# Attention beside a feed-forward product: the keys in chunks of 128 with 64 left over, and the left-over ones in four quadrants of the tensor engine

## The chip, the cores and the metric

One core of one Trainium2 chip. The metric is the device time of one execution in microseconds (us), medians of several runs. Where two kernels are compared, the ratio is the mean time of the one's fast runs over the mean of the other's fast runs in the same rounds, so it is not quite the ratio of the medians quoted.

## The reference, cut to what matters

```python
q, k, v: (8, 12, 448, 64)                      # batch, heads, sequence, head size; all float32
q_n, k_n = rmsnorm(q, g_q), rmsnorm(k, g_k)
attn = softmax(q_n @ k_n.T / sqrt(64))         # 448 x 448 for each head
x = (attn @ v) arranged to (3584, 768)
h = x @ w_in                                   # first product, to 2048 columns
out = relu(h)**2 @ w_out                       # second product, back to 768
```

## The kernel before

Two batches make a span, four spans in all; a span has twelve pairs of heads. The attention of span 0 runs alone. The attention of each later span runs beside the second product of the span ahead of it: Python generators deal out the matmuls of both, in one order for the tensor engine (PE). These three stretches are what the change touches. The products use a scheme with seven multiplications in place of eight, for which VectorE also forms sums and differences ("combine"). In span 0 it does so during the first eight products of the stretch.

The parts that matter, cut:

```python
NJ, SP = 4, 112                                   # 448 keys = 4 chunks of 112

def scores(i, c):                                 # later spans; keys on the partitions
    sc = ps_s.tile([SP, 2, 512], F32, tag="s")    # PSUM: 2 x 2 banks
    for h in range(2):                            # two heads, two row tiles of 64
        nc.tensor.matmul(sc[:, h, 0:S], qkT[rows(h), 0, 1, chunk c], qkT[rows(h), 0, 0, :])
    nc.scalar.activation(probs[i, c], sc[:, :, 0:S], AF.Exp)

def values(i):
    pavs[i] = ps_o.tile([P, S], F32, tag="o")     # one bank
    for c in range(NJ):
        for h in range(2):                        # two heads, two column tiles of 64
            nc.tensor.matmul(pavs[i][rows(h), :], vs[i][:, h, c, :], probs[i, c][:, h, :], ...)

def attention(first):                             # one turn for each pair, beside the second product
        scores(i, 0); scores(i, 1)
        values(i - 1)
        spread(i - 1)                             # ScalarE's queue: load the factors back, 1/sum of each query
        add_up(i, 1)                              # VectorE: row sums, chunk on chunk
        scores(i, 2); scores(i, 3)
        norm_by_squares(i + 2); yield             # VectorE and GpSimd
        transposes(i + 1); yield
        add_up(i, 2); add_up(i, 3)
        finish(i - 1); yield                      # VectorE: x = values * factors; frees bank "o"
        fold(i)                                   # VectorE: sum over partitions, reciprocal
        combine_x(i - 1); yield
        nc.sync.dma_start(factors in DRAM, ...)   # SyncE's queue: store the factors
        yield

# second product, one output block of eight matmuls:
ps = ps_o.tile([P, S], F32, tag="t") if j % 3 == 2 else bank("ps")    # three banks in turn
```

All eight PSUM banks are in use: four for the scores, "o" for the values, and "t" and two of `bank` for the second product.

## Time and profile before

| | |
|---|---|
| time, median of the first four runs | 1403.36 us |
| span in the profile | 1399.7 us |
| TensorE busy | 99% at a mean granted clock of 0.998 |
| the three stretches beside the second product | 207.4 us each |

A stretch is read from the trace: from the first score matmul of its twelve pairs to the first matmul of the next first product. The table of stretches has it as follows (length; then busy time of PE, PEld, DVE, ACT, POOL, each with its count; granted clock, DMA share, GB/s):

```profile
263.22:470.64 207.42, 207.42 (x721) 90.94 (x721) 159.53 (x303) 59.13 (x73) 83.76 (x42) 1.00 0.54 116
597.37:804.78 207.41, 207.41 (x721) 90.94 (x721) 144.18 (x275) 58.02 (x72) 82.85 (x43) 1.00 0.54 116
931.51:1138.93 207.42, 207.42 (x721) 90.94 (x721) 145.24 (x275) 57.91 (x72) 83.98 (x43) 1.00 0.51 111
```

PE is busy for the whole of each; no wait shows. VectorE (the third busy time) has 15 us more to do in the first, the combinations.

### The profile page before, as it was taken

The page shows a single profiled execution, that of the slowest core. Times are in us where ns is not written, and L with a number is a line of the kernel's source. Part 1 is how long each engine was busy: PE and PEld are TensorE (multiplying, and loading weights), DVE is VectorE, ACT ScalarE, POOL GpSimd, SP SyncE. Part 2 cuts the span into 40 slices and gives each one's busy share as a digit, 9 for nine tenths or more (in the row PEclk, how much of TensorE's full clock was granted, in tenths as well). Part 3 has the DMA queues.
Part 4 walks back from the last instruction along what each step waited for, and adds up shares of the span by engine and source line. Part 5 has one row for each costly group of instructions (what it writes and reads, how often), then busy time and mean ns, then how long its engine had stood idle before and what let it go on. Part 6 is the DMA issues. An engine that isn't in the chain of part 4 may idle for free.

```text
span 1399.7 us, 14445 instructions
## 1 busy us (share of the span) xinstructions
PE 1379.2 (99%) x4450; PEld 638.5 (46%) x4450; DVE 802.2 (57%) x1398; ACT 419.6 (30%) x621; POOL 581.7 (42%) x400
## 2 busy tenths in 40 slices
PE   8989999999999999999999999999999999999997
PEld 3333455444444454544444455444444445554553
DVE  6889676589876234476777523457777633332111
ACT  7875556432322011233332011233333201110000
POOL 5998877444552123544453122544445302221000
PEclk9999999999999999999999999999999999999999
DMA  9687998545764332344665333344564332334443
GB/s 240 189 229 199 341 384 306 143 97 120 144 121 105 102 90 85 104 113 110 127 130 119 97 94 90 98 106 105 129 126 102 95 101 85 90 87 104 106 111 70
DMA packets 430915, 188.79 MB, mean 135 GB/s; under 512 B 277484, under 2 KB 428780, under 8 KB 430828
## 3 DMA queue, kind: packets, MB, share of 16 engines
q1 hardware_dynamic: 421228, 179.05, 49.8%
q10 hardware_dynamic: 9472, 8.72, 2.3%
q8 instruction: 38, 0.62, 0.2%
q14 instruction: 49, 0.40, 0.1%
q0 software_dynamic: 128, 0.00, 0.0%
HBM read 154.54 MB, written 33.16 MB: 134 GB/s over the span
## 4 chain that ended last, share of the span: by engine, by line
PE 93%; POOL 3%; DVE 1%; DMA 1%; ACT 1%; issue 1%; ACTq 0%; POOLq 0%
PE ps L1047 37%; PE sc L749 10%; PE pd L1000 10%; PE pa L1000 10%; PE pc L1000 10%; PE pav L805 9%; PE pb L1000 5%; PE tot L819 1%; POOL rstd L697 1%; POOL gC L563 1%; DMA sw<-w1s 1%; POOL gC L569 1%; PE pt L737 0%; ACT gT L754 0%; POOL qk L699 0%
## 5 line engine op out<-in xcount | busy, mean ns | idle before, releaser
L1047 PE MATMUL ps<-gT,sw 128*128 128x448 f32 x768 | 299.2, 543 | 0.8 <-POOL gT L977 0.8
L719 POOL TENSOR_TENSOR half<-half,mhalf 128x28 f32<-128x28 f32 x36 | 173.6, 4822 | 266.9 <-DVE half L718 226.8
L1047 PE MATMUL ps<-gC,sw 128*128 128x448 f32 x576 | 225.2, 543 | 0.0
L977 POOL TENSOR_TENSOR gT<-gT 128x448 f32<-128x448 f32 x96 | 94.9, 990 | 309.9 <-ACT gT L973 309.9
L1047 PEld LDWEIGHTS ps<-gT,sw 128*128 128x128 f32 x768 | 144.1, 190 | 150.7 <-issue 147.0
L756 ACT ACTIVATE pr<-sc 112x896 f32<-112x896 f32 x120 | 104.7, 914 | 293.4 <-PE sc L749 184.9
L749 PE MATMUL sc<-qkT 64*112 64x448 f32 x768 | 170.6, 563 | 0.9 <-ACT qkT L383 0.8
L1047 PEld LDWEIGHTS ps<-gC,sw 128*128 128x128 f32 x576 | 108.2, 190 | 112.1 <-issue 110.8
L1000 PE MATMUL pa<-xT,sw 128*128 128x448 f32 x384 | 154.9, 540 | 0.0
L973 ACT ACTIVATE gT<-gT 128x448 f32<-128x448 f32 x96 | 55.3, 577 | 310.1 <-DVE gT L1015 310.0
L749 PEld LDWEIGHTS sc<-qkT 64*112 64x112 f32 x768 | 61.2, 173 | 97.9 <-issue 81.3
L1000 PEld LDWEIGHTS pa<-xT,sw 128*128 128x128 f32 x384 | 73.0, 190 | 71.6 <-issue 70.3
L805 PE MATMUL pav<-pr,vt 112*64 112x448 f32 x480 | 100.2, 547 | 0.0
L721 POOL TENSOR_TENSOR qk<-qk,half 128x448 f32<-128x448 f32 x72 | 81.3, 1150 | 2.8
L764 DVE TENSOR_TENSOR acc<-acc,pr 112x896 f32<-112x896 f32 x60 | 68.2, 1136 | 21.0 <-ACT pr L756 18.5
L1000 PE MATMUL pb<-xC,sw 128*128 128x448 f32 x192 | 77.6, 540 | 1.5 <-issue 1.5
L1000 PE MATMUL pd<-xT,sw 128*128 128x448 f32 x192 | 77.9, 542 | 0.0
L1000 PE MATMUL pc<-xC,sw 128*128 128x448 f32 x192 | 77.5, 540 | 0.2 <-DMA sw<-w1s 0.2
L1000 PE MATMUL pd<-xC,sw 128*128 128x448 f32 x192 | 77.5, 540 | 0.0
L1000 PE MATMUL pc<-xT,sw 128*128 128x448 f32 x192 | 77.4, 539 | 0.0
L1015 DVE TENSOR_TENSOR gT<-z,pd 128x448 f32<-128x448 f32 x32 | 19.8, 620 | 99.7 <-PE pd L1000 99.7
L569 POOL TENSOR_TENSOR gC<-gC 128x384 f32<-128x384 f32 x64 | 72.8, 1157 | 2.5
(120 smaller groups left out, 1551.0 us busy)
## 6 DMA issues: line engine op xcount, KB each, us to landing
sw<-w1s SPq DMA_DIRECT2D x224, 192.0 KB, 2.3
sw<-w2s SPq DMA_DIRECT2D x168, 256.0 KB, 3.3
w1s<-gC SPq DMA_DIRECT2D x8, 1344.0 KB, 7.5
w2s<-gC SPq DMA_DIRECT2D x8, 1344.0 KB, 7.6
out_dram<-osb SPq DMA_DIRECT2D x184, 56.0 KB, 1.9
qk<-in_q_dram SPq DMA_DIRECT2D x144, 56.0 KB, 3.0
qk<-in_k_dram SPq DMA_DIRECT2D x144, 56.0 KB, 2.9
vt<-in_v_dram SPq DMA_DIRECT2D x72, 112.0 KB, 2.9
```

Source lines behind the costliest of these rows:

```text
L569: nc.gpsimd.tensor_tensor(*[blocks_of(n)[:, i] for i in (dst, x, y)], op)
L719: nc.gpsimd.tensor_tensor(half, half, mhalf, ALU.pow)
L721: nc.gpsimd.tensor_tensor(qkn[:, s], raw[:, s], half[:, s * NG:(s + 1) * NG].rearrange("p g -> p g ()").to_broadcast([P, NG, 32]), ALU.mult)
L749: nc.tensor.matmul(sc[:, h, 0:S], qkT[rows, at, 1, c * SP:(c + 1) * SP], qkT[rows, at, 0, :], start=True, stop=True)
L756: nc.scalar.activation(pr, sc[:, :, 0:S], AF.Exp)
L764: nc.vector.tensor_tensor(acc, probs[i, 0] if c == 1 else acc, probs[i, c], ALU.add)
L805: nc.tensor.matmul(pavs[i][h * D:(h + 1) * D, :], vs[i][:, h, c, :], probs[i, c][:, h, :], start=(c == 0), stop=(c == NJ - 1))
L973: nc.scalar.activation(g, src, AF.Relu)
L977: nc.gpsimd.tensor_tensor(g, g, g, ALU.mult)
L1000: nc.tensor.matmul(ps, stream[n + i][:, c], rhs[:, c], start=first and c == 0, stop=c == HC - 1, skip_group_check=not first)
L1015: add(g, x, ps, ALU.add)
L1047: nc.tensor.matmul(ps, stream[n][:, c % 4], rhs_of[i][:, c], start=c == 0, stop=c == HF - 1)
```

## The change

The intent: 4 chunks of 112 keys leave rows of the array empty. Three full chunks of 128 and a rest of 64 need fewer steps, if the rest costs half a step: its 64 keys by 64 values fill a quarter of the array, so two heads times two halves of the queries can run at once in the four quadrants. The halves of the queries land on two row tiles, and their values in two banks, so the second half has a bank ("t") of its own and is joined to the first later. The diff, cut (asserts, loads and buffer sizes left out):

```diff
 def load_v(i):
-    for h in range(2):
-        nc.sync.dma_start(vs[i][:, h], v[b, h0 + h].rearrange("(j p) d -> p j d", j=NJ))
+    for h in range(2):
+        nc.sync.dma_start(vs[i][:, h, 0:NF], v[b, h0 + h, 0:NF * P].rearrange("(j p) d -> p j d", j=NF))
+    for rows in sides:        # the last 64 keys twice, on partitions 0-63 and 64-127
+        nc.sync.dma_start(vs[i][rows, :, NF], v[b, h0:h0 + 2, NF * P:].rearrange("h p d -> p h d"))
 def scores(i, c):
+    n = S if c < NF else S // 2
+    for h in range(2):
+        for m in range(S // n):
+            part = slice(0, P) if c < NF else sides[m]
+            nc.tensor.matmul(sc[part, h, 0:n], qkT[rows, 0, 1, c * P:min((c + 1) * P, S)],
+                             qkT[rows, 0, 0, m * n:(m + 1) * n], start=True, stop=True)
 def add_up(i, c):
+    if i >= NAT and c == NF:
+        for m, rows in enumerate(sides):
+            part = acc[rows, :, m * S // 2:(m + 1) * S // 2]
+            nc.vector.tensor_tensor(part, part, probs[i, c][rows], ALU.add)
+        return
+def later_values(i):          # after the three full chunks
+    rests[i] = ps_o.tile([P, S], F32, tag="t", name="rest")
+    for h in range(2):
+        for m, rows in enumerate(sides):
+            into = rests[i] if m else pavs[i]
+            nc.tensor.matmul(into[h * D:(h + 1) * D, 0:S // 2], vs[i][rows, h, NF, :],
+                             probs[i, NF][rows, h, :], start=bool(m), stop=True)
 def finish(i):
+    half = pav[:, S // 2:]
+    nc.vector.tensor_tensor(half, half, rests.pop(i), ALU.add)
     nc.vector.tensor_tensor(x, pav, factors, ALU.mult)
 def attention(first):
-    scores(i, 2)
-    scores(i, 3)
+    scores(i, 3)
+    scores(i, 2)
+    nc.scalar.copy(rest, rests[i - 1][:, 0:S // 2])
 # second product
-    ps = ps_o.tile([P, S], F32, tag="t", name="ps") if j % 3 == 2 else bank("ps")
+    ps = bank("ps")
```

## The prediction

> **What bounds the kernel now.** I read the page's engine rows first, then the 40 slices, the chain that ended last, the timeline of TensorE, and last the timeline of ScalarE where an eviction was late.
>
> ```profile
> PE 1379.2 (99%) x4450; PEld 638.5 (46%) x4450; DVE 802.2 (57%) x1398; ACT 419.6 (30%) x621; POOL 581.7 (42%) x400
> ```
>
> ```profile
> PE  8989999999999999999999999999999999999997
> ...
> PEclk9999999999999999999999999999999999999999
> ```
>
> TensorE is busy for 1379.2 of 1399.7 us at full clock, and after the first few slices never idle. The chain that ended last is 93% PE. So only TensorE time counts, plus any wait that the change newly puts in front of TensorE. The change touches the stretches in which attention for the next two batches runs between the matmuls of the second product (L1047): three stretches of 12 head pairs. One such period, from the timeline of TensorE (start, length, engine, line, operation, count):
>
> ```profile
> 643.93 1.76 PE L749 MATMUL sc<-qkT 64*112 64x448 f32 x8
> 645.62 2.48 PE L805 MATMUL pav<-pr,vt 112*64 112x448 f32 x12
> 647.93 0.92 PE L805 MATMUL pav<-qkT,vt 112*64 112x448 f32 x4
> 648.78 1.76 PE L749 MATMUL sc<-qkT 64*112 64x448 f32 x8
> 650.47 7.03 PE L1047 MATMUL ps<-gT,sw 128*128 128x448 f32 x18
> 657.34 3.17 PE L1047 MATMUL ps<-gC,sw 128*128 128x448 f32 x8
> 660.44 1.76 PE L749 MATMUL sc<-qkT 64*112 64x448 f32 x8
> ```
>
> From start to start: scores of chunks 0 and 1 take 645.62 - 643.93 = 1.69 us, values 648.78 - 645.62 = 3.16, scores of chunks 2 and 3 1.69, the 26 records of L1047 9.97. Every matmul leaves two records. Read record by record, starts in steady state are 0.3757 us apart for 448 columns. In the scores (64 rows, two row tiles) and the values (64 columns, two column tiles) the two heads' records start 5 to 7 ns apart, so a pair costs one step of 0.3757. Take those steps off and a fixed part is left where the shape of the tiles changes: scores 1.69 - 4 x 0.3757 = 0.19, values 3.16 - 8 x 0.3757 = 0.15, L1047 9.97 - 26 x 0.3757 = 0.20.
>
> **What the Trainium skill says.** (1) "FP8 and Floating Point Precision", TensorE Precision Notes: true FP32 takes four passes through the array. The trace agrees: two records of 0.3757 us for 448 columns, 0.75 us a matmul. (2) "TensorEngine Tiling (Array Packing)", Tiling Modes, Key Properties: changing the tiling mode drains TensorE, changing the tile does not, and a 64x64 mode has four independent tiles. The trace has the drain, 0.15 to 0.20 us a change; no run here yet has the four tiles. (3) "TensorE: Matmul & The Clock Gate", Part 3: Packing small matmuls: tiles start about 4 ns apart and run at once. The trace shows 5 to 7 ns for two tiles. (4) "PSUM — Partial Sum Buffer", PSUM bank collisions raise a hardware error: different row tiles may not write one bank at the same time. No run shows it, but it is why the change needs a bank of its own for the second half of the queries.
>
> **The change, part by part.** Beside the second product the 448 keys go as 3 x 128 + 64 instead of 4 x 112.
>
> *Removed:* one of four chunks, in scores and in values: 2 x 2 steps of 0.3757 = 1.503 us of a pair's 6.01.
>
> *Added:* the 64 keys left over, in scores and in values, as four matmuls of 64x64x224, one to a quadrant. If all four run at once, a set is two steps of 224 columns, about 0.3757/2 = 0.189 us each: 0.378 us a set, 0.756 for both. The weight loads of 64 columns took 136 ns in the values, less than a step of 189, so they should hide as now.
>
> *Mode changes:* the order is scores 0 and 1 (64x128), values 0 to 2 (128x64), left-over values and then left-over scores (both 64x64, hence the swap of chunks 2 and 3), scores 2 (64x128), L1047. That is five changes in place of four: about +0.15 us, as for the other 64-column mode.
>
> So a period with both parts: -1.503 + 0.756 + 0.15 = -0.60 us. 11 such periods a stretch, 33 in all: -19.7 us. The first pair of a stretch has scores alone and the last period values alone: each -0.752 + 0.378 + 0.15 = -0.22, six in all, -1.3. **Together -21.0 us on TensorE.**
>
> *Other engines.* VectorE: the last addition becomes two of 64 partitions by 448, at 0.62 each (the mean of its 128x448 additions) in place of one of about 1.12, +0.1; joining the halves, 224 wide, is 0.39 by the slope between 448 (0.617) and 896 (1.081). So +0.5 us a period. ScalarE: an exponential of half the size saves about 0.37, a copy of 224 columns costs about as much (both estimates from its 448-wide rows of 0.53 to 0.58). GpSimd loses three clears of 0.84. SyncE issues two more transfers of v per pair, near 0.5 us each. None is on the chain unless it delays something for TensorE:
>
> ```profile
> 268.37:453.00 184.63, 184.63 (x647) 80.70 (x647) 151.44 (x290) 55.67 (x69) 82.05 (x39) 1.00 0.55 118
> 602.52:787.50 184.98, 184.98 (x647) 80.90 (x648) 135.19 (x260) 55.13 (x69) 80.63 (x39) 1.00 0.55 117
> ```
>
> (The table of stretches: length, then busy time of PE, PEld, DVE, ACT, POOL.) VectorE was busy for 151 of 185 us in the first stretch and would be for about 157 of 178: 89%, not a bound on the mean.
>
> *Moved: a bank.* The products of L1047 rotated over three banks and now have two, since the third ("t") holds the left-over values. A product of eight matmuls is 6.0 us of TensorE, so an eviction must now be over before the next product ends, not the one after. For all 84 products I compared the end of the eviction with the start of the product two later. Nearly all have 2 to 12 us to spare. Three do not, the same product (the fifth) in each stretch, because its copy is on ScalarE:
>
> ```profile
> 321.56 1.11 ACTq L785 DMA_DIRECT2D xT<-factors  x2
> 322.78 1.72 ACT L756 ACTIVATE pr<-sc 112x896 f32<-112x896 f32 x2 [7.87 <-PE ps L1047]
> 324.39 0.54 ACT L1056 COPY p<-ps 128x448 f32<-128x448 f32 x1
> ```
>
> ```profile
> 654.39 1.11 ACTq L785 DMA_DIRECT2D xT<-factors  x2
> 655.60 1.72 ACT L756 ACTIVATE pr<-sc 112x896 f32<-112x896 f32 x2 [8.84 <-issue]
> 657.21 0.54 ACT L1056 COPY p<-ps 128x448 f32<-128x448 f32 x1
> ```
>
> ScalarE stood some 8 us ahead of these transfers of the factors. The copies end at 324.93 and 657.75; the products two later start at 323.19 and 657.34 (the L1047 line above). With two banks TensorE would have waited 1.7 and 0.4 us, and with periods 0.6 us shorter 2.3 and 1.0. In the third stretch 1.0 us was to spare, 0.4 would be left. I charge **+3.4 us**.
>
> The sum: 1403.6 - 21.0 + 3.4 = **1386 us**, 1.3% faster.
>
> **The rivals.**
>
> *A: the quadrants do not run four at a time.* Each of the four matmuls has two records on its own quadrant, and the second must follow the first. If the queue does not look past three waiting second passes, the tiles start one after another: five steps of 0.189 a set in place of two, +0.57 us, times 72 sets = +41 us: 1427 us. If only two run together, four steps, +0.38, +27 us: 1413. One at a time, eight steps, +1.13, +82: 1468. For it: each column half reads its own stream from the same rows and no trace here has four tiles; 16 loads and matmuls must start in 0.38 us, four times as densely as in the values. Against it: with two tiles the first pass of the second head starts 5 ns after that of the first head and ahead of its second pass, in row and in column tiles alike, and the transposes (L737) start a load and a matmul every 94 ns, which is their array time. I give the cases of A together about 15%.
>
> *B: a wait takes the place.* VectorE goes near its limit in the first stretch, lags, and holds up the two banks, or ScalarE delays the exponentials that free the scores' banks. For it: 89% busy, and a late eviction now stops TensorE. Against: at the score banks the trace leaves about 2.7 us between the end of an exponential and the matmul that needs its bank, and the new order takes only 0.2 to 0.6 of it. B would make 5 to 12 us of waits instead of 3.4: 1388 to 1395.
>
> *C: no waits and cheap changes of mode:* 1403.6 - 21.0 = 1382.6, or 1380 with a smaller drain.
>
> **The range and the chances.** The mechanism alone gives 1383, the bank 1386, B up to 1395, the mild half of A about 1400. Range 1381 to 1401. Over 2% faster means under 1375.5, which even all the removed work without a new change of mode (36 x 0.75 = 27 us, 1376.7) does not reach: 3%. Over 2% slower means above 1431.7, only with quadrants run nearly in turn: 4%. Within 2%: 93%.
>
> **What would show each step right or wrong.** In the timeline of TensorE: the left-over values as eight records over about 0.4 to 0.55 us from their start to that of the left-over scores, and those about 0.38 us to the start of scores 2; record starts in fours a few ns apart. If they start in twos or singly, A holds. The L1047 records keep their 0.3757 us, and a period falls from 16.5 to 15.9 us (15.76 to 15.16 with 24 records). Idle time of TensorE ahead of L1047, released by ScalarE's copy L1056's counterpart, of 2 to 4 us in all shows the lost bank; more, or released by VectorE, shows B. The prediction is wrong in its mechanism if the three stretches together do not shorten by 15 to 22 us.

## The result, and the profile after

| | before | after |
|---|---|---|
| median (first four runs) | 1403.36 us | 1393.22 us (1391.20 to 1396.39) |
| ratio, 95% interval | | 0.9935 (0.9911 to 0.9959) |
| span in the profile | 1399.7 us | 1389.0 us |

The time lies in the range, 7 us above the central value. The page's first row and the table of stretches, after:

```profile
PE 1360.9 (98%) x4738; PEld 636.1 (46%) x4738; DVE 829.7 (60%) x1470; ACT 418.0 (30%) x657; POOL 572.1 (41%) x397
```

```profile
263.59:470.79 207.20, 201.93 (x818) 89.92 (x818) 170.03 (x327) 58.13 (x85) 82.01 (x41) 1.00 0.55 118
597.48:799.73 202.25, 201.14 (x817) 90.11 (x817) 153.66 (x299) 57.65 (x84) 79.06 (x42) 1.00 0.55 121
926.44:1127.97 201.53, 201.15 (x818) 90.16 (x818) 153.64 (x299) 57.70 (x84) 79.86 (x42) 1.00 0.52 116
```

The three stretches came from 622.3 to 611.0 us, 11.3 shorter: 0.2 in the first, 5.2 in the second, 5.9 in the third. So the question is why the first gained nothing.

The timeline of PE shows that the quadrants work (start, length, engine, line, operation, shapes, count):

```profile
678.52 1.67 PE L834 MATMUL pav<-pr,vt 128*64 128x448 f32 x8
680.13 0.40 PE L840 MATMUL pav<-half,vt 64*64 64x224 f32 x1
680.13 0.40 PE L840 MATMUL rest<-half,vt 64*64 64x224 f32 x1
680.14 0.40 PE L840 MATMUL pav<-half,vt 64*64 64x224 f32 x1
680.15 0.40 PE L840 MATMUL rest<-half,vt 64*64 64x224 f32 x1
680.37 0.35 PE L840 MATMUL pav<-half,vt 64*64 64x224 f32 x1
...
680.56 1.51 PE L758 MATMUL sc<-qkT 64*64 64x224 f32 x12
682.00 5.53 PE L1089 MATMUL ps<-gT,sw 128*128 128x448 f32 x14
```

Four records start within 20 ns (5 to 7 ns apart, read record by record), then the four second passes together, and 0.19 us later the left-over scores begin, with no change of tile shape between. An undisturbed turn of attention (scores, values, left-over keys, without L1089) takes 5.98 us; before it took 6.54.

Where the rest went, in the first stretch. Two kinds of waits are new. The first stands ahead of the values:

```profile
308.92 1.77 PE L758 MATMUL sc<-qkT 64*128 64x448 f32 x8
312.83 1.73 PE L834 MATMUL pav<-pr,vt 128*64 128x448 f32 x8 [2.14 <-DVE xT L877]
```

In square brackets is the idle time and what ended it: the multiplication that empties the values' bank for the pair two turns back. VectorE (DVE) at that time:

```profile
307.92 1.08 DVE L784 TENSOR_TENSOR acc<-acc,qkT 128x896 f32<-128x896 f32 x1
309.04 2.65 DVE L782 TENSOR_TENSOR acc<-acc,half 64x448 f32<-64x448 f32 x2
311.72 0.40 DVE L876 TENSOR_TENSOR pav<-pav,half 128x224 f32<-128x224 f32 x1
312.16 0.62 DVE L877 TENSOR_TENSOR xT<-pav,xT 128x448 f32<-128x448 f32 x1
```

It works without a gap, one instruction after another: it is simply late. GpSimd (POOL) at that time:

```profile
304.11 4.80 POOL L724 TENSOR_TENSOR half<-half,mhalf 128x28 f32<-128x28 f32 x1 [11.47 <-DVE half L723]
308.99 2.22 POOL L726 TENSOR_TENSOR qk<-qk,half 128x448 f32<-128x448 f32 x2
```

The same place in the kernel before, where the multiplication (L839) ended 0.55 us before the values began:

```profile
308.75 1.64 DVE L764 TENSOR_TENSOR acc<-acc,qkT 112x896 f32<-112x896 f32 x1
310.32 0.61 DVE L839 TENSOR_TENSOR xT<-pav,xT 128x448 f32<-128x448 f32 x1
```

```profile
311.48 0.97 PE L805 MATMUL pav<-pr,vt 112*64 112x448 f32 x4
```

After the change the scores behind the values in the same turn were late too, by some 0.6 us in all. They wait for ScalarE's exponentials, which free their banks; and these had waited for a step of `fold` on VectorE (L793):

```profile
315.01 1.73 ACT L761 ACTIVATE pr<-sc 128x896 f32<-128x896 f32 x2 [6.22 <-DVE quarters L793]
```

```profile
316.79 1.02 PE L758 MATMUL sc<-qkT 64*128 64x448 f32 x4 [0.20 <-ACT pr L761]
```

The second kind is ahead of the seventh product, for its bank:

```profile
322.86 1.13 ACTq L805 DMA_DIRECT2D xT<-factors  x2
...
325.55 0.57 ACT L1098 COPY p<-ps 128x448 f32<-128x448 f32 x1
```

```profile
326.21 3.25 PE L1089 MATMUL ps<-gC,sw 128*128 128x448 f32 x8 [1.44 <-POOL half L724]
```

The bracket names GpSimd, but the copy on ScalarE ends at 326.12 and the matmul starts 0.1 us later, in each of the three stretches: that is the bank it waits for.

To weigh the waits I took each turn and each block of L1089 in the trace and subtracted its undisturbed length (5.98 us a turn; 0.3757 us a record plus 0.20 a block). The first stretch waits 2.84 and 1.73 us in the turns in which the values were late (the idle time ahead of the values alone is 2.14 and 1.03; some 0.6 of each lies ahead of the scores that follow) and 1.68 for the bank; the second 1.38 and the third 0.65 for the bank. With trifles, 8.4 us in all. Without them each stretch is 200.87 us, so TensorE was spared 3 x 6.55 = 19.6 us, and 19.6 - 8.4 = 11.2.

### The profile page after: what moved, and what is told of

It is laid out like the page before. It is cut to its first block, busy times and chain, and to the rows that moved or that the text cites. A ratio compares the mean times of both kernels' runs of the same rounds, so it can differ in the third digit from the quotient of the medians.

```text
span 1389.0 us, 15124 instructions
## 1 busy us (share of the span) xinstructions
PE 1360.9 (98%) x4738; PEld 636.1 (46%) x4738; DVE 829.7 (60%) x1470; ACT 418.0 (30%) x657; POOL 572.1 (41%) x397
## 4 chain that ended last, share of the span: by engine, by line
PE 85%; DVE 6%; POOL 3%; issue 2%; DMA 2%; ACT 2%; SPq 1%; ACTq 0%; POOLq 0%
PE ps L1089 33%; PE pd L1042 10%; PE pa L1042 10%; PE pc L1042 10%; PE sc L758 7%; PE pav L834 5%; PE pb L1042 5%; PE sc L767 1%; PE pav L840 1%; PE tot L854 1%; PE pav L826 1%; POOL rstd L702 1%; DMA sw<-w1s 1%; POOL gC L566 1%; DMA factors<-square 1%
## 5 line engine op out<-in xcount | busy, mean ns | idle before, releaser
L1089 PE MATMUL ps<-gT,sw 128*128 128x448 f32 x768 | 299.2, 543 | 0.8 <-POOL gT L1019 0.8
L724 POOL TENSOR_TENSOR half<-half,mhalf 128x28 f32<-128x28 f32 x36 | 173.6, 4822 | 267.6 <-DVE half L723 249.3
L1089 PE MATMUL ps<-gC,sw 128*128 128x448 f32 x576 | 225.5, 543 | 2.9 <-ACT p L1098 1.5
L1089 PEld LDWEIGHTS ps<-gT,sw 128*128 128x128 f32 x768 | 144.1, 190 | 149.3 <-issue 145.2
L1089 PEld LDWEIGHTS ps<-gC,sw 128*128 128x128 f32 x576 | 107.9, 190 | 115.8 <-issue 108.4
L758 PE MATMUL sc<-qkT 64*128 64x448 f32 (+1 forms) x720 | 118.8, 484 | 0.7 <-ACT pr L761 0.4
L761 ACT ACTIVATE pr<-sc 128x896 f32<-128x896 f32 x87 | 77.3, 914 | 133.1 <-DVE quarters L793 62.1
L834 PE MATMUL pav<-pr,vt 128*64 128x448 f32 x348 | 74.2, 548 | 3.2 <-DVE xT L877 3.2
L726 POOL TENSOR_TENSOR qk<-qk,half 128x448 f32<-128x448 f32 x72 | 74.2, 1051 | 2.8
L758 PEld LDWEIGHTS sc<-qkT 64*128 64x128 f32 (+1 forms) x720 | 46.2, 165 | 54.3 <-issue 42.9
L1049 DVE TENSOR_TENSOR z<-p,pb 128x448 f32<-128x448 f32 x32 | 19.8, 619 | 82.4 <-PE pb L1042 82.4
```

Of the source, the lines that this page charges most:

```text
L724: nc.gpsimd.tensor_tensor(half, half, mhalf, ALU.pow)
L726: nc.gpsimd.tensor_tensor(qkn[:, s], raw[:, s], half[:, s * NG:(s + 1) * NG].rearrange("p g -> p g ()").to_broadcast([P, NG, 32]), ALU.mult)
L758: nc.tensor.matmul(sc[part, h, 0:n], qkT[rows, 0, 1, c * P:min((c + 1) * P, S)], qkT[rows, 0, 0, m * n:(m + 1) * n], start=True, stop=True)
L761: nc.scalar.activation(pr, sc[:, :, 0:n], AF.Exp)
L834: nc.tensor.matmul(pavs[i][h * D:(h + 1) * D, :], vs[i][:, h, c, :], probs[i, c][:, h, :], start=(c == 0), stop=False)
L1049: add(z, p1, ps, ALU.add)
```

## The experiments

Each kernel ran beside the kernel before on one chip; three sets (e1 to e4, e5 to e8, e9 to e11). Medians of the kernel before were 1401.91, 1401.87 and 1402.25 us. All results of the traces first, lengths of the three stretches and the waits in them, as worked out above:

| kernel | median, us | ratio to before (95%) | stretches, us | waits, us |
|---|---|---|---|---|
| before | | | 207.42, 207.42, 207.42 | 0.0 |
| the change, first profile | | | 207.20, 202.25, 201.53 | 8.4 |
| e1 the change again | 1392.01 | 0.9926 (0.9913 to 0.9938) | 207.07, 201.72, 201.43 | 7.6 |
| e2 before, two banks | 1406.05 | 1.0024 (1.0011 to 1.0037) | 209.16, 207.43, 207.42 | 1.7 |
| e3 no last additions | 1386.42 | 0.9885 (0.9870 to 0.9900) | 202.18, 200.87, 200.87 | 1.3 |
| e4 finish first | 1400.54 | 0.9993 (0.9979 to 1.0007) | 209.03, 205.36, 202.97 | 14.7 |
| e5 factors on ScalarE's queue | 1388.52 | 0.9890 (0.9876 to 0.9903) | 204.21, 201.80, 200.87 | 4.3 |
| e6 no swap | 1394.67 | 0.9944 (0.9929 to 0.9958) | 207.38, 203.60, 203.26 | 6.3 |
| e7 skewed dealing | 1388.76 | 0.9903 (0.9884 to 0.9923) | 204.91, 201.65, 201.25 | 5.2 |
| e8 e5 and e7 | 1389.94 | 0.9917 (0.9898 to 0.9936) | 207.02, 201.72, 200.87 | 7.0 |
| e9 e5 and early dealing | 1385.03 | 0.9878 (0.9863 to 0.9892) | 201.73, 201.89, 200.87 | 1.9 |
| e10 the change again | 1391.71 | 0.9928 (0.9915 to 0.9940) | 207.05, 202.01, 201.27 | 7.7 |
| e11 e5 again | 1388.71 | 0.9902 (0.9888 to 0.9916) | 204.22, 201.72, 200.87 | 4.2 |

For e6 the waits are without 33 x 0.16 us for the additional change of shape.

Sets e5 to e8 had no control of their own: the change is compared there by the ratios to the kernel before. The stretches tell more than the whole time of one run: the part ahead of the first stretch, in which these kernels are alike, lasted from 261.5 to 268.1 us in these traces.

### e1: the change again

> The changed kernel once more, as the control of this set. Its four runs so far spread from 1391.2 to 1396.4 us, while in its trace TensorE work fell by 19.6 us in the three stretches and 8.4 us of new waits came: 3.7 us ahead of the product two after the late copy (lost bank), 4.65 us in the first stretch ahead of the values (two waits of 2.8 and 1.7 us, for the values' bank). Theory (both waits are steady): 10 to 12 us faster than before, 0.992 to 0.993, with the same two kinds of waits in the trace. Rival (the waits are chance of one run): the waits differ in place or size by more than 1 us.

Measured: 0.9926, and the same waits at the same two places; but the first one was 3.85 us, not 2.84. The table of stretches around it (same columns as above):

```profile
305.00:311.45 6.45, 6.45 (x18) 3.01 (x16) 6.19 (x15) 3.10 (x5) 4.79 (x1) 1.00 0.68 146
311.45:315.37 3.92, 1.78 (x10) 0.69 (x9) 3.79 (x6) 0.00 (x0) 2.22 (x2) 1.00 0.33 89
315.37:319.85 4.48, 4.48 (x21) 1.46 (x25) 4.25 (x10) 1.73 (x2) 0.00 (x0) 0.62 0.00 0
```

After PE had stood for 2.14 us the granted clock (third figure from the right) is 0.62: the trace has it at half for 3.41 us from 316.3. Half a clock for 3.41 us is 1.7 us of work. The turn was only 1.0 longer than in the first profile, since the 0.6 us of waits behind the values were taken up. In the first profile and in e10, idle times of the same 2.14 us were not followed by it; in e6, e7 and e8, with 2.2, 2.1 and 3.2 us, it came too. "TensorE: Matmul & The Clock Gate", Part 1: The HAM clock gate, states that the clock halves after at least one idle window of some 3.4 us and that the windows run free of the kernel; the trace agrees with the 3.41 us and with the half rate, and that only one of three profiles shows it would fit windows that run free, though PE's idle here was only 2.14 us. By the letter two waits meet the rival's mark of 1 us: this one, and the first one for the bank, 0.57 against 1.68. e10, a third profile, has 2.84, 1.71 and 1.56 again. The waits are steady in place, and sizes and the clock vary by a microsecond or two: the theory stands, with that limit.

### e2: the kernel before with two banks

```diff
-ps = ps_o.tile([P, S], F32, tag="t", name="ps") if j % 3 == 2 else bank("ps")
+ps = bank("ps")
```

> The kernel before, with the products of L1047 turned over two banks in place of three and nothing else changed. Theory (the lost bank costs by the late copy on ScalarE alone): the fifth product's successor waits 1.7 us in the first stretch and 0.4 in the second, none in the third, so +2.1 us (1.0015). Rival 1 (two banks are enough, the waits in the changed kernel come from elsewhere): 0. Rival 2 (two banks hurt at other products too): +5 us or more, with waits at several places.

Measured: one wait of 1.74 us, in the first stretch, ahead of the seventh product, and nothing else: the 1.7 us that the trace of before had foretold. The 0.4 of the second stretch did not come. The whole time rose by 0.24% (0.11 to 0.37), 3.4 us (1.5 to 5.2), of which the trace shows 1.7. Rivals 1 and 2 fall: the lost bank costs by itself, but little, and at that product alone.

### e3: without the additions of the left-over chunk

```diff
 add_up(i, 2)
-add_up(i, 3)
```

> The changed kernel without the two half-height additions of the left-over chunk on VectorE beside the second product; the row sums then lack 64 keys, so the result is wrong on purpose. Theory (VectorE's load holds the values' bank in the first stretch): the waits of 2.8 and 1.7 us ahead of the values vanish; the waits for the late copy stay at about 3 to 4 us; so 4 to 5 us under the control. Rival (the values wait for the factors' transfer, not for VectorE's queue): these waits stay, and the time with them.

Measured: 1386.42 us, 5.6 under e1. Both waits ahead of the values are gone, and of the others only 1.3 us is left, in the first stretch; the second and third run at 200.87 without any. That is more than the theory said: the late copy too is in part VectorE's lateness. Its load is the cause, and the rival (the factors' transfer alone) falls. The result was wrong, as intended.

### e4: finish first

```diff
+if i > first:
+    finish(i - 1)
 if i < last:
     add_up(i, 2)
     add_up(i, 3)
-if i > first:
-    finish(i - 1)
```

> The changed kernel with the last step of the pair before (joining the halves and scaling, which frees the values' bank) put ahead of the additions of chunks 2 and 3 in VectorE's queue. Nothing is added or removed. Theory (the bank comes free late because of VectorE's order): the two waits ahead of the values vanish, 4 to 5 us under the control. Rival (that step then waits for the factors' transfer and stops VectorE, so other things are late): the waits ahead of the values go but others of 2 us or more appear in each stretch at the fifth product, and the time is that of the control or worse.

Measured: slower than the change by 8.5 us. The values no longer wait, but the left-over scores after them do, for an exponential that was late because `fold`, behind the same VectorE queue, was late:

```profile
315.45 0.61 PE L758 MATMUL sc<-qkT 64*64 64x224 f32 x8 [1.68 <-ACT pr L761]
```

And at the end of each stretch VectorE now stands for the factors with the additions and evictions behind it:

```profile
446.78 0.40 DVE L876 TENSOR_TENSOR pav<-pav,half 128x224 f32<-128x224 f32 x1 [3.00 <-ACT half L968]
447.96 0.62 DVE L877 TENSOR_TENSOR xT<-pav,xT 128x448 f32<-128x448 f32 x1 [0.78 <-DMA xT<-factors]
```

The rival holds, though not at the place that it named: its waits of 2.2, 3.3 and 1.6 us stood at the end of the three stretches, and those for the bank at the fifth product's successor were 1.2, 1.1 and 0.4. So a better order was not to be had this way: the step that waits for a transfer does harm ahead of others.

### e5 and e11: the factors' store on ScalarE's queue

```diff
 values(i - 1)
+nc.scalar.dma_start(sums["out"][(i - 1) % 2], sums["square"][0:2 * S // 32, 1])
 spread(i - 1)
 ...
-nc.sync.dma_start(sums["out"][i % 2], sums["square"][0:2 * S // 32, 1])
```

> The changed kernel with the small store of the factors taken off SyncE's queue, where it stood behind the transfers of results, and issued on ScalarE's queue just ahead of the loads that read it back. Theory (the fifth product's copy is late because ScalarE stands behind those loads, and they behind SyncE's queue): the waits ahead of the product two after it (0.6 to 1.7 us in each stretch, 2 to 3.7 in all) vanish, stretches 2 and 3 come down to 200.9 us, the first keeps its 4.6 us of waits ahead of the values; 2 to 3.5 us under the control. Rival (the copy is late for another reason, or ScalarE now waits for the store's landing just as long): the stretches stay at 201.5 to 202.2.

> The factors' store on ScalarE's queue alone, again, beside the control on one chip. If its gain over the changed kernel is steady: 0.989 of the kernel before, 3 to 5 us under the control, the stretches 204, 201.8 and 200.9. Rival (its earlier lead was the chip or chance): within 1 us of the control.

Measured: 0.9890, and 0.9902 when repeated, against 0.9926 (e1, of another set) and 0.9928 (e10, of the same set as the repeat) for the change: 5.0 and 3.6 us less by the ratios, 3.5 and 3.0 by the medians. The bank's waits are gone. ScalarE, from e5's timeline:

```profile
320.97 0.31 ACTq L961 DMA_DIRECT2D factors<-square  x1
323.27 1.10 ACTq L805 DMA_DIRECT2D xT<-factors  x2
...
326.23 0.57 ACT L1097 COPY p<-ps 128x448 f32<-128x448 f32 x1
```

The store leaves 1.5 us after the turn's first exponential started (319.47), the load 2.3 us behind it, and the copy starts 5.3 us after that store began and ends 0.6 later. The seventh product needed its bank at 329.07 and had it. In the change the store had stood behind four transfers of results on SyncE. The wait of 2.84 us ahead of the values stayed, as expected; the one of 1.73 went. One miss: a wait of 0.9 us came late in the second stretch (0.4 in the first), which no run followed up. The trace of e5 shows where it comes from: from 766 us on SyncE's queue stood 5.8 us ahead of a load of values (L685) until the moved store had landed. The load of the second product's weights behind it was issued at 776.15, and PE, idle for 0.69 us, went on at 779.50, 3.3 us later, which is what the page of the change gives for such a load from issue to landing. (The bracket there names VectorE's L1102, which frees the bank of the product just ended, not the one that starts.)

### e6: without the swap

```diff
-scores(i, 3)
-scores(i, 2)
+scores(i, 2)
+scores(i, 3)
```

> The changed kernel with the scores of chunk 2 before those of the left-over keys again, so the two sets of four quadrants are no longer neighbours. Theory (every change of tile shape drains TensorE, as read in the trace): one more change in 33 periods at 0.15 to 0.19 us, +5 to +6 us; a period without waits goes from 5.98 to about 6.15 us. Rival (the swap is of no account, the cost of a change hides): 0.

Measured: a turn takes 6.14 us in place of 5.98 in every period, +0.16 for the one additional change of tile shape. The second and third stretch are 1.8 us longer than e1's, 11 x 0.16. The first is 0.3 longer, since its waits took up the difference. So +4.0 us in the trace; the whole time says +2.5 against e1's ratio, with intervals as wide as that. The swap is worth what the drain says; the rival falls.

### e7 and e8: the second product dealt out unevenly in the first stretch

```diff
-while done < min(total, total * (u + 1) // (10 * NPAIR + 1)):
+x = min(1.0, (u + 1) / (10 * NPAIR + 1))
+if span == 0:
+    x += 0.25 * x * (1 - x)
+while done < min(total, int(total * x + 1e-6)):
```

> The changed kernel with the matmuls of the second product dealt out unevenly in the first stretch alone: a quarter more beside each early pair, a quarter fewer beside each late one, the sum as before. No engine gets less work in all. Theory (VectorE has too much to do in the first five periods only, where it also forms the combinations of the second product): the waits of 4.6 us ahead of the values fall to under 2, 3 us or more under the control; stretches 2 and 3 unchanged. Rival (the wait is of the chain through the factors, which a longer period does not shorten, or the late periods become too short): the waits stay or move to the end of the stretch.

> Both of the last two edits that add nothing: the factors' store on ScalarE's queue, and the uneven dealing in the first stretch. Theory: nearly all waits gone, every stretch within 1 us of 200.9, so 19 us of the 19.6 that TensorE was spared reach the time: 5 to 7 us under the control and 17 to 19 under the kernel before (0.987 to 0.988). Rival: new waits take their place, and the gain over the control is under 3 us.

Measured: the early waits are gone in both, with no work taken off any engine: they were a matter of VectorE's load in the early periods. But one of 4.0 us came at the end of the first stretch (5.2 in e8), where the last pair's factors are waited for while the products come closer together:

```profile
456.95 0.62 DVE L877 TENSOR_TENSOR xT<-pav,xT 128x448 f32<-128x448 f32 x1 [1.47 <-DMA xT<-factors]
...
459.95 0.61 DVE L1108 TENSOR_TENSOR p<-p,ps 128x448 f32<-128x448 f32 x1
```

```profile
460.62 5.72 PE L1089 MATMUL ps<-gT,sw 128*128 128x448 f32 x10 [2.07 <-DVE p L1108]
```

The clock was at half for 3.41 us from 461.2 on top. By the ratios e7 still gained about 3 us on the change (e1), though the two intervals overlap; e8, expected to be best, gained 1.3, inside the noise: my theory of it was wrong, its rival right.

### e9 and e10: early dealing, with the factors' store; and the control

```diff
+if span == 0 and x < 0.85:
+    x = 1.25 * x if x < 0.35 else 0.85 - 0.825 * (0.85 - x)
```

> The factors' store on ScalarE's queue, and in the first stretch a quarter more of the second product beside the early third of the pairs, made good in the middle, with the last pairs as in the changed kernel. Theory: the even skew failed only because it squeezed the end of the stretch, where the last pair's factors are waited for; so the early waits stay away and the late ones of 4 to 5 us do not come: the first stretch 201.5 to 203 us, 1 to 3 us under the factors' store alone, 5 to 6 under the changed kernel. Rival (any dealing moves the wait to another place): the first stretch stays at 204 or more and nothing is gained over the factors' store alone.

> The changed kernel again, for comparison on the same chip. By the control before, 0.9926 of the kernel before; stretches of about 207.1, 202 and 201.5 us.

Measured: 1385.03 us, 0.9878 of the kernel before, against 0.9928 for the change on the same chip; correct. The first stretch is 201.73 us, and 1.9 us of waits are left in all three. This version beats both kernels: 17.1 us (15 to 19) of the 19.6 that TensorE was spared reach the time.

## Why the prediction was right or wrong, point by point

- **TensorE is the bound, and only the three stretches change.** Right: the other parts lie within 0.4 us of each other in the two profiles.
- **Four quadrants at once.** Right. Rival A falls: record starts come in fours, a set of two passes of 224 columns at 0.19 us each.
- **-21.0 us on TensorE.** Near: measured -19.6. The mis-sized term is the additional change of mode: 0.15 assumed, 0.19 by the turn (5.98 less 12 x 0.3757 and 4 x 0.189 leaves 0.72 for four changes, where 6.54 less 16 x 0.3757 left 0.53 for three), 0.16 by e6.
- **+3.4 us for the bank.** Right in place, the same product in each stretch. The sum is near partly by luck: 3.7 us in the first profile, but as 1.7, 1.4 and 0.65 against 2.3, 1.0 and none, and 2.0 and 3.1 in the two controls. e2 shows the lost bank alone at 1.7; e5 that the store's place in SyncE's queue is a cause, e3 that VectorE's lateness is another. The reading "Three do not" missed a fourth place, the end of the second stretch, with 1.3 us to spare (797.50 to 798.77); e4 waited there.
- **Rival B, VectorE, left out of the sum.** This is the step that failed: the charge for "None is on the chain unless it delays something" was zero and measured 4.6 us. The rival itself foresaw a late VectorE and 5 to 12 us of waits in all (8.4 measured), but at the second product's two banks and the scores' banks, not at the values'. Two things were wrong in its working (besides a slip: 157 of 178 is 88%).

  First, the two half-height additions were put at 0.62 us each, +0.1 a period. In the first profile they take 0.62 where GpSimd is idle or raises to a power (L724), but 1.26 on average and up to 1.37 under GpSimd's multiplications (L726), as 18 of the 72 are: 2.65 a pair in the late turn above, against 1.27 in a later one. VectorE's busy time in the first stretch rose by 10.5 us, where +0.5 a period makes 6. "SBUF — State Buffer", Who interferes with whom, states that a VectorE instruction with two SBUF inputs contends with a GpSimd one that reads SBUF. The trace agrees for L726, and the instructions with one SBUF input, such as the transpose (L792), keep their 1.10 under it; but L724 reads SBUF too, and under it the additions keep their 0.62. The link to GpSimd is read from the trace: no run took GpSimd's work away. The mean that was used (0.617, that of L839, which reads PSUM and keeps its time beside GpSimd) could not show it; the trace of before could, in the 1.64 us of L764 above.

  Second, the margins were checked for the scores' banks and for the second product's, not for the values' bank; and for the scores by a typical 2.7 us, where the two places in the first stretch at which the scores then waited had 0.53 and 0.16 us to spare in the trace of before (ahead of the scores at 314.63 and 347.65). At the values' bank, in the trace of before, the multiplication ended at 310.93 and the values began at 311.48, 0.55 us to spare, which an addition 1 us longer uses up.

  e3 and e7 show that VectorE's load in the early periods is the cause; the one other order tried, e4, did not help.
- **The number.** -19.6 + 3.7 + 4.6 = -11.3, the measured stretches; predicted -17.6. The chances and the range hold; of the 6.3 us that the centre was off, 4.6 are this term, 1.4 the drain and 0.3 the bank. The range held because it was wide enough for rival B. By its own test the prediction failed: the stretches were to shorten by 15 to 22 us, and did by 11.3. TensorE's own part of that, 19.6, lies inside; the test put work and waits together.
- **Its remark on float32.** The two records a matmul do not by themselves show four passes; no sum rests on it.

## What to carry to other kernels

When a change shortens the periods of a bound engine, list every buffer that this engine waits for and compare the margin of each with what the change adds to the engine that frees it, in the busiest period and not in the mean. An instruction's duration from a mean row may double beside another engine's work (0.62 to 1.26 us here); look it up at the place where it will run. And work that was spared may be had back without sparing more: here a store moved to another queue and a few matmuls dealt out earlier were worth 0.5% (e9 against e10).

## What the Trainium skill lacked or had wrong

- "TensorEngine Tiling (Array Packing)" says that a change of mode drains TensorE but not what it costs: 0.15 to 0.20 us a change in the kernel before, 0.16 in e6.
- That page lists a 64x64 mode with four tiles, but neither it nor "TensorE: Matmul & The Clock Gate" has a measurement of it with float32: they ran at once, starts 5 to 7 ns apart, two passes of 224 columns at 0.19 us.
- "TensorE: Matmul & The Clock Gate" advises against idle gaps over some 3 us: in e1 a gap of 2.14 us was followed by the half clock for 3.41 us, in two other profiles of the same kernel it was not.
- "SBUF — State Buffer" says of two-input VectorE instructions beside a GpSimd one that reads SBUF that the one that starts first holds the ports for the whole instruction and the other fully blocks. Here such an addition went from 0.62 to 1.26 us on average and 1.37 at most under L726, but the 36 that ran under L724 alone, an instruction of 4.8 us that also reads SBUF, kept 0.62 (spans on GpSimd are rough).
- No page has a measurement of a VectorE addition over 64 partitions beside one over 128: both took 0.62 us for 448 columns.
